# First scores of the attention between the last products of the projections, and two transfers moved behind the first key loads

## The chip, the cores and the metric

The kernel runs on one core of one Trainium2 chip. The metric is the device time of one execution in microseconds (us); the kernel before takes 1719.75 us as the median of three runs (1718.42 to 1723.87). The engines work at the same time and are tied to each other by semaphores: PE (TensorE) multiplies, DVE (VectorE) and ACT (ScalarE) read its results out of the PSUM banks, POOL (GpSimd) does element-wise work in SBUF, and SP (SyncE) issues the transfers. A transfer goes through one queue, in the order in which SP issues it.

## What is computed

One transformer block with modulated layer norms, attention over 32 heads of 16 columns, and a GELU layer, on 2048 rows of 512 columns in float32:

```python
mod = (silu(c) @ w_mod)            # six rows of 512: sa, ca, ga, sb, cb, gb
h = layernorm(x) * (1 + ca) + sa
qkv = h @ wqkv                      # q, k, v: 32 heads x 16 columns each
p = softmax((q @ k.T) * 16**-0.5)   # per head, 2048 x 2048
x = x + ga * ((p @ v) @ wo)
h = layernorm(x) * (1 + cb) + sb
x = x + gb * (gelu(h @ w1 + b1) @ w2 + b2)
```

The softmax is taken with the true maximum of each row, so every score is computed twice: once to find the row's maximum, once to take the exponential. Operands are split into an upper and a lower part, so that a product consists of several matrix multiplications.

## The kernel before, in words

**The stages.** A first stage (to about 69 us of the profile) normalises and transposes the four blocks `b` of 512 rows and makes the first products: the keys and queries of the first column group (`k = 0`) of each block, and some of the values. A second stage, the loop over `n` (L721 to L790), makes the other products (35 items: values, then keys and queries of column groups 1 to 3) with the row maxima of the first nine units woven in. A unit `u` is four heads times 512 rows of queries. The third stage, the loop over `s` (L1013 to L1035), is the attention: 32 units of 16 steps. A step has four scores (`X0` to `X3`, `exp_step`), each followed by an exponential on ACT, four products with the values (`P`, `pv_step`, of the step before), and three maxima of later units (`M`, `max_bank`). The last stage is the GELU layer.

**The first maxima.** In the second stage a maximum is found in pairs: `kd` holds for the key blocks 0 and 2 the keys themselves and for blocks 1 and 3 the difference to the block before. A `V` slot multiplies queries with the difference, ACT takes the relu (L579, tile `cp`), and a `U` slot multiplies the same queries with the keys; DVE adds both and keeps the extreme (L582). Each visit of the loop does one `V` and one `U`; about 0.68 visits fall on a step `i` of the loop. Units 0 and 1 take turns of eight slots: slots 0 to 7 use unit 0's queries with key blocks 0 and 1, slots 8 to 15 those of unit 1, and from slot 16 key blocks 2 and 3 are wanted.

**What feeds them.** `proj_qk` splits a product and hands back `rest`, which stores the parts to DRAM: `store(qk_d...)`, and for the keys of `k = 0` also `store(kd_d...)` (L464). `load_qm(u)` brings a unit's queries into a tile `qmx` by six transfers of 64 KB (L515); `build_k` brings keys into `kts[0]` by six transfers (L504). SP issues in the order of the program: at the start of block 3 it has the stores of block 2 (`qk`, `kd`, `qk`), then `load_qm(0)`, `build_k` for key blocks 0 and 1, `load_qm(1)`, then a store of values, the stores of block 3, and at `n = 0` `build_k` for key blocks 2 and 3. Eight semaphores go round over the transfers, so a transfer is issued only when the eighth before it has landed.

**The seam between the second and the third stage.** The product of an item is worked off in halves of 64 rows; the second half runs `LAG = 6` steps behind, so that for `n = N` (N = 35) and the first six steps of `n = N + 1` only second halves and maxima are left. `evacuate(N - 1)` copies the last product out (ACT, tile `raw`, L446). After that the pools of the stage are closed (`wcm`, `hcm`, `tcm`), the banks are dealt out anew (`set_rings`), `ppool` is opened, in whose tiles `p` the exponentials go, loads of keys are issued, and `epool` is opened with the loads of `ga_b` and `gb_b` (L812). Then step `s = 0` begins: `X0` to `X3` and no maxima.

**What sets the order.** All of this is written out by hand: each engine executes its instructions in the order of the program.

## Time and profile before

| | us |
|---|---|
| median of 3 runs | 1719.75 |
| lowest and highest run | 1718.42, 1723.87 |
| the profiled execution's own time | 1728.43 |
| its span, first to last instruction | 1726.7 |
| PE busy | 1715.8 |
| DVE busy | 1389.9 |
| ACT busy | 1352.9 |
| POOL busy | 312.7 |

The times of day in the text are us from the start of the span. A row of the timeline gives the start, the length, the engine, the line, the operation, the tile written and the tile read, and how many instructions were merged (`x6`); in brackets stands how long the engine idled before it and what ended that. `SPq` is SP issuing a transfer. A row of busy time by stretch gives for each engine the busy us and the number of instructions (`x`), then the clock that TensorE was granted (1.00 is full), the share of time in which the transfer engines were busy, and GB/s. PE's ends of matmuls are modelled, so that PE looks busy in nearly every stretch; how much it gets done is read from counts.

### The profile page before, as it was taken

Reading aid. Unit: us, or ns where it says so; the run is one execution under the profiler, and the core shown is the slowest. Engines: PE = TensorE matmul, PEld = TensorE weight load, DVE = VectorE, ACT = ScalarE, POOL = GpSimd, SP = SyncE. Lnnn points to the kernel's source line nnn. Section 1 sums busy time; section 2 is a strip of 40 time slices with the busy share of each in tenths; the row PEclk is TensorE's granted clock in tenths of the full one; section 3 lists DMA queues with packets and bytes.
Section 4 is the critical chain, followed back from the end, with each engine's and each line's share of the span. In section 5 each row is a group of like instructions: output and inputs, shape, how many; then the busy total and the mean of one; then the engine's idle time right before and its main releaser. Section 6 shows DMA issues by size and latency. Waiting matters only on the chain.

```text
span 1726.7 us, 29970 instructions
## 1 busy us (share of the span) xinstructions
PE 1715.8 (99%) x10968; PEld 905.6 (52%) x10968; DVE 1389.9 (80%) x2559; ACT 1352.9 (78%) x2580; POOL 312.7 (18%) x341
## 2 busy tenths in 40 slices
PE   9999999999999999999999999999999999999998
PEld 7766664333443334333433343334433488888887
DVE  6699997998888888888888888888885296746453
ACT  3588888999999999999999999999999632222222
POOL 3205430110000000000000000000022154636562
PEclk9899998999999999999999999999999999999999
DMA  9854988314112201400500110111023064423331
GB/s 328 223 124 153 172 177 162 73 41 60 40 36 44 55 24 33 69 23 24 88 23 23 43 33 24 39 32 27 23 66 106 19 204 131 138 79 110 99 122 49
DMA packets 125223, 144.22 MB, mean 84 GB/s; under 512 B 39026, under 2 KB 74866, under 8 KB 123124
## 3 DMA queue, kind: packets, MB, share of 16 engines
q1 hardware_dynamic: 123828, 139.71, 32.6%
q10 hardware_dynamic: 1248, 2.59, 0.4%
q8 instruction: 86, 1.41, 0.4%
q14 instruction: 61, 0.50, 0.1%
HBM read 106.37 MB, written 35.87 MB: 82 GB/s over the span
## 4 chain that ended last, share of the span: by engine, by line
PE 95%; DVE 2%; ACT 1%; SPq 1%; DMA 1%; issue 1%; POOL 0%; ACTq 0%
PE pv L843 30%; PE mx L554 20%; PE sc L1010 14%; PE sc L308 9%; PE mx L1074 6%; PE mx L573 5%; PE sc L776 4%; PE pv L1074 2%; PE sc L950 2%; PE sc L773 2%; PE mx L950 1%; PE sc L261 0%; PE sc L359 0%; DMA wmod<-in_w_mod_dram 0%; DVE bst L239 0%
## 5 line engine op out<-in xcount | busy, mean ns | idle before, releaser
L1011 ACT ACTIVATE p<-sc 128x512 f32<-128x512 f32 x2048 | 1054.7, 613 | 43.1 <-PE sc L1010 16.8
L556 DVE TENSOR_REDUCE mxs<-mx 128x1 f32<-128x512 f32 x1472 | 928.1, 683 | 118.8 <-PE sc L1010 91.4
L843 PE MATMUL pv<-p,vg 128*32 128x512 f32 x4096 | 548.1, 607 | 0.0
L1010 PE MATMUL sc<-qst,kq 50*128 50x512 f32 x1024 | 286.8, 438 | 0.3 <-ACT raw L446 0.3
L1010 PE MATMUL sc<-qst,kt 50*128 50x512 f32 x1024 | 282.5, 432 | 0.0
L554 PE MATMUL mx<-kq,qmx 48*128 48x512 f32 x768 | 262.5, 428 | 0.5 <-DVE mxs L556 0.4
L554 PEld LDWEIGHTS mx<-kq,qmx 48*128 48x128 f32 x768 | 121.9, 184 | 230.4 <-DVE mxs L556 212.1
L554 PE MATMUL mx<-kt,qmx 48*128 48x512 f32 x704 | 241.1, 430 | 0.0
L554 PEld LDWEIGHTS mx<-kt,qmx 48*128 48x128 f32 x704 | 113.6, 186 | 211.0 <-DVE mxs L556 191.5
L1053 ACT ACTIVATE g<-sc,b_c 128x512 f32<-128x512 f32 x56 | 38.6, 690 | 223.0 <-PE sc L308 218.5
L595 POOL CAST m<-mn 128x16 fp32r<-128x16 f32 x32 | 6.3, 198 | 1040.8 <-DVE mn L589 1040.8
L582 DVE CUSTOM_DVE_ANT_0 cp<-mx,cp 128x512 f32<-128x512 f32 x288 | 182.1, 686 | 14.0 <-PE mx L573 11.2
L573 PE MATMUL mx<-kt,qmx 48*128 48x512 f32 x576 | 181.1, 428 | 2.9 <-DMA qmx<-qk 1.2
L579 ACT ACTIVATE cp<-mx 128x512 f32<-128x512 f32 x288 | 157.2, 603 | 26.2 <-PE mx L573 20.9
L843 PEld LDWEIGHTS pv<-p,vg 128*32 128x32 f32 x4096 | 81.1, 108 | 181.3 <-issue 169.7
L1010 PEld LDWEIGHTS sc<-qst,kq 50*128 50x128 f32 x1024 | 126.8, 186 | 30.3 <-ACT p L1011 21.3
L573 PEld LDWEIGHTS mx<-kt,qmx 48*128 48x128 f32 x576 | 102.5, 190 | 57.7 <-DVE mxf L582 34.3
L1057 DVE TENSOR_TENSOR glo<-g,ghi 128x512 fp32r<-128x512 f32 x56 | 57.6, 1029 | 92.1 <-ACT ghi L1056 92.1
L1010 PEld LDWEIGHTS sc<-qst,kt 50*128 50x128 f32 x1024 | 125.6, 185 | 9.4 <-ACT p L1011 2.4
L879 POOL TENSOR_TENSOR w1l<-w1r,w1h 128x512 fp32r<-128x512 f32 x56 | 76.5, 1366 | 146.7 <-DVE w1h L878 123.1
L881 POOL TENSOR_TENSOR w2l<-w2r,w2h 128x512 fp32r<-128x512 f32 x56 | 82.5, 1473 | 6.2 <-DVE w2h L880 5.8
L308 PE MATMUL sc<-kt,w1h 128*128 128x512 f32 x224 | 73.8, 391 | 0.0
(185 smaller groups left out, 1912.5 us busy)
## 6 DMA issues: line engine op xcount, KB each, us to landing
qk<-parts SPq DMA_DIRECT2D x30, 512.0 KB
w1r<-in_B_w_dram SPq DMA_DIRECT2D x56, 256.0 KB
w2r<-in_B_w_dram SPq DMA_DIRECT2D x56, 256.0 KB
qmx<-qk SPq DMA_DIRECT2D x192, 64.0 KB
qst<-qk SPq DMA_DIRECT2D x192, 64.0 KB
kq<-qk SPq DMA_DIRECT2D x24, 256.0 KB
kt<-qk SPq DMA_DIRECT2D x24, 256.0 KB
vg<-v SPq DMA_DIRECT2D x8, 664.0 KB
```

What stands on the lines that cost most here:

```text
L308: te.matmul(ps, p, q, start=i == 0, stop=i == len(terms) - 1)
L554: te.matmul(ps, qmx[u][rows, p, qc * P : (qc + 1) * P], kst[u // NB][rows, p, kr * TB : (kr + 1) * TB], start=True, stop=True)
L556: ve.tensor_reduce(mxs[u][:, p, a, qc, kr : kr + 1], ps, axis=AX.X, op=ALU.max, negate=True)
L573: te.matmul(ps, qmx[u][rows, p, qc * P : (qc + 1) * P], kd[u // NB][rows, p, t0 : t0 + TB], start=True, stop=True)
L579: ac.activation(vpos[n, a], ps, AF.Relu)
L582: ve.tensor_tensor_reduce(v, ps, v, -1.0, 3.0e38, ALU.add, ALU.min, mxs[u][:, p, a, qc, r : r + 1])
L843: te.matmul(cur_pv[0][32 * j : 32 * (j + 1)], vg[g][:, kc, j * VW : j * VW + 32], pt.pop((s, j)), start=kc == 0, stop=kc == NKC - 1)
L879: gp.tensor_tensor(alo, a, ahi.bitcast(F32), op=ALU.subtract)
L881: gp.tensor_tensor(blo, b, bhi.bitcast(F32), op=ALU.subtract)
L1010: te.matmul(ps, k[r0 : r0 + KX, p, kc * P : (kc + 1) * P], q[r0 : r0 + KX, p], start=True, stop=True)
L1011: ac.activation(pb, ps, AF.Exp, scale=SCALE)
L1074: te.matmul(acc[qb][t], p[:, sl], q, start=f == 0 and n == 0, stop=f == NF - 1 and n == 2)
```

## The change

Front: the store of block 2's keys to `kd_d[0]` is kept in a list `late` and issued with block 3's keys; `load_qm(1)` is taken from before the second stage to `n = 0`, ahead of the second `build_k`.

Seam: the four scores and exponentials of attention step 0 are issued inside the second stage's last two rounds, at steps 9 and 11 of `n = N` and steps 1 and 3 of `n = N + 1`. The tiles of `ppool` don't exist yet there, so these four go to a new tile `px` and to three tiles of the projections that are free by then (`pm`, two halves of `wraw`). Because of this `tcm` is closed later: `epool` is opened, with its two loads, after attention step 1. The bank of the last product is taken out of the ring, and the rings are dealt out in another order. Step 0 of the attention loop then issues no scores.

```diff
+FIRST_X = (9, 11, 13, 15)
...
         def rest():
             store(qk_d[w][k], parts)
-            if pair and b % 2 == 0:
+            if pair and b == 2 and not k:
+                late.append(lambda: store(kd_d[k], parts))
+            elif pair and b % 2 == 0:
                 store(kd_d[k], parts)
             elif pair:
+                while late and not k:
+                    late.pop(0)()
...
             load_qm(0)
             build_k(kts[0], kd_d[0], 0, 0, 2 * TB)
-            load_qm(1)
...
         if n == 0:
+            load_qm(1)
             build_k(kts[0], kd_d[0], 0, 2 * TB, S)
...
+        if n == N:
+            wraw = tpool.tile([P, 2, KC, P], F32, tag="wraw", name="p_w", bufs=1).rearrange("p a k n -> p a (k n)")
+            pm = tpool.tile([P, TB], F32, tag="pm", name="p_m", bufs=1)
+            pxcm, pxpool = pool("pxpool")
+            px = pxpool.tile([P, TB], F32, name="px")
+            first_p.extend([px, pm, wraw[:, 0], wraw[:, 1]])
...
                 acc[n] = bank()
+                if n == N - 1:
+                    last_sc = rings["sc"].pop()
...
+            if n >= N and (n - N) * NT + i in FIRST_X:
+                exp_step(0, FIRST_X.index((n - N) * NT + i))
...
-    close(tcm)
...
-    set_rings(sc=(sc[0], sc[1], mx[0], sc[2]), mx=mx[1:4], pv=mx[4:])
+    set_rings(sc=(sc[0], mx[0], sc[1], last_sc), mx=mx[1:4], pv=mx[4:])
...
-    epool = ctx.enter_context(tc.tile_pool(name="epool", bufs=1, side="right"))
+    def open_epool():
+        nonlocal epool, wo_hi, wo_lo, x2a, b2_b, ga_b, gb_b, o_b, xn_b
+        close(tcm)
+        epool = ctx.enter_context(tc.tile_pool(name="epool", bufs=1, side="right"))
...
+    at(1, open_epool)
...
             if tok[0] == "X":
-                exp_step(s, int(tok[1]))
+                if s:
+                    exp_step(s, int(tok[1]))
```

`exp_step` itself is moved up in the file and takes its tile from `first_p` for step 0. `build_k` loses an unused argument.

More of the change, by code (lines that the diff above doesn't have):

```diff
@@ L311, in block_kernel @@
     st = [ac]
+    late = []
     def first_block():
@@ L497, in heads, with build_k @@
         return ap.rearrange("(p a d) t -> a d p t", a=2, d=DH)[a]
-    def build_k(dst, src, g, t0=0, t1=S, parts=(0, 1, 2)):
-        for i in parts:
+    def build_k(dst, src, g, t0=0, t1=S, eng=sy):
+        for i in range(3):
             part = (0, 0, 1)[i]
@@ L503, in build_k @@
                 r0 = a * 64 + i * DH
-                sy.dma_start(dst[r0 : r0 + DH, :, t0:t1].bitcast(F32), heads(src, g, part, a, t0, t1))
+                eng.dma_start(dst[r0 : r0 + DH, :, t0:t1].bitcast(F32), heads(src, g, part, a, t0, t1))
     def load_k(g, tile):
@@ L540, in one_rows, with exp_step @@
             sy.dma_start(k[r0 : r0 + 2].bitcast(F32), one_d[:, None, :].to_broadcast([2, 2, S]))
+    pt, first_p = {}, []
+    def exp_step(s, j):
+        u, kc = divmod(s, NKC)
+        q, k = qst[u], kst[u // NB]
+        p, a = divmod(j, 2)
+        ps = bank()
+        pb = pt[s, j] = ppool.tile([P, TB], F32, tag="p", name="p", bufs=10) if s else first_p[j]
+        r0 = a * 64
+        te.matmul(ps, k[r0 : r0 + KX, p, kc * P : (kc + 1) * P], q[r0 : r0 + KX, p], start=True, stop=True)
+        ac.activation(pb, ps, AF.Exp, scale=SCALE)
     mxs, left, vpos = {}, {}, {}
@@ L702, in block_kernel @@
     led, todo = 0, []
-    new, late = [], []
+    new = []
     def visit():
@@ L804, in block_kernel @@
     load_k(3, kq[1])
-    epool = ctx.enter_context(tc.tile_pool(name="epool", bufs=1, side="right"))
-    wo_hi = epool.tile([P, KC, D], FR, name="wo_hi")
-    wo_lo = epool.tile([P, KC, D], FR, name="wo_lo")
-    x2a = [epool.tile([P, 4, D], F32, name=f"x2a{i}") for i in range(2)]
-    b2_b, ga_b, gb_b = [epool.tile([P, D], F32, name=n) for n in ("b2_b", "ga_b", "gb_b")]
-    for i, t in enumerate((ga_b, gb_b)):
-        sy.dma_start(t, bass.AP(tensor=g_d.tensor, offset=g_d[i].offset, ap=[[0, P], [1, D]]))
-    o_b = epool.tile([P, 4, D], F32, name="o_b")
-    xn_b = epool.tile([P, 4, D], F32, name="xn_b")
+    epool = wo_hi = wo_lo = x2a = b2_b = ga_b = gb_b = o_b = xn_b = None
+    def open_epool():
+        nonlocal epool, wo_hi, wo_lo, x2a, b2_b, ga_b, gb_b, o_b, xn_b
+        close(tcm)
+        epool = ctx.enter_context(tc.tile_pool(name="epool", bufs=1, side="right"))
+        wo_hi = epool.tile([P, KC, D], FR, name="wo_hi")
+        wo_lo = epool.tile([P, KC, D], FR, name="wo_lo")
+        x2a = [epool.tile([P, 4, D], F32, name=f"x2a{i}") for i in range(2)]
+        b2_b, ga_b, gb_b = [epool.tile([P, D], F32, name=n) for n in ("b2_b", "ga_b", "gb_b")]
+        for i, t in enumerate((ga_b, gb_b)):
+            sy.dma_start(t, bass.AP(tensor=g_d.tensor, offset=g_d[i].offset, ap=[[0, P], [1, D]]))
+        o_b = epool.tile([P, 4, D], F32, name="o_b")
+        xn_b = epool.tile([P, 4, D], F32, name="xn_b")
     wo_r = {}
@@ L823, in wo_load @@
             sy.dma_start(b2_b, bass.AP(tensor=b2.tensor, offset=b2.offset, ap=[[0, P], [1, D]]))
-    pt = {}
     def attn_out(u, pv):
@@ L1000, in block_kernel @@
         at(base + n, lambda i=i: run("l", lambda: ln2(0), i))
-    def exp_step(s, j):
-        u, kc = divmod(s, NKC)
-        q, k = qst[u], kst[u // NB]
-        p, a = divmod(j, 2)
-        ps = bank()
-        pb = pt[s, j] = ppool.tile([P, TB], F32, tag="p", name="p", bufs=10)
-        r0 = a * 64
-        te.matmul(ps, k[r0 : r0 + KX, p, kc * P : (kc + 1) * P], q[r0 : r0 + KX, p], start=True, stop=True)
-        ac.activation(pb, ps, AF.Exp, scale=SCALE)
     for s in range(NS):
@@ L1036, in block_kernel @@
     pv_step(NS - 1)
-    for cm in (pcm, qcm, vgcm, kqcm, qmcm):
+    for cm in (pcm, pxcm, qcm, vgcm, kqcm, qmcm):
         close(cm)
```

## The prediction

> **What bounds the kernel now.** First the page: busy time, the slices with the granted clock, the chain that ended last by engine.

> ```profile
> span 1726.7 us, 29970 instructions
> ...
> PE 1715.8 (99%) x10968; PEld 905.6 (52%) x10968; DVE 1389.9 (80%) x2559; ACT 1352.9 (78%) x2580; POOL 312.7 (18%) x341
> ...
> PEclk9899998999999999999999999999999999999999
> ...
> PE 95%; DVE 2%; ACT 1%; SPq 1%; DMA 1%; issue 1%; POOL 0%; ACTq 0%
> ```

> PE ends nearly all of the chain, so time is lost where PE waits or runs slowly. The clock line has three slices that aren't 9: the start, the second (43 to 86 us) and the seventh (259 to 302 us). The change touches just these last two places. Busy time by stretch, cut where the granted clock changes (columns: stretch, length, then PE, PEld, DVE, ACT and POOL busy with instruction counts, clock, transfer share, GB/s):

> ```profile
> 67.41:70.82 3.41, 2.25 (x10) 1.34 (x9) 0.69 (x1) 1.46 (x4) 1.73 (x2) 1.00 0.92 140
> 70.83:84.47 13.64, 13.64 (x52) 11.24 (x51) 7.84 (x23) 8.17 (x15) 0.00 (x0) 0.50 0.89 228
> 84.48:98.12 13.64, 13.43 (x104) 9.16 (x103) 12.82 (x41) 11.96 (x23) 0.00 (x0) 1.00 0.40 109
> 265.39:268.79 3.40, 3.10 (x16) 1.33 (x15) 2.29 (x10) 3.40 (x8) 1.72 (x4) 1.00 0.79 290
> 268.80:279.03 10.23, 10.23 (x45) 3.88 (x37) 5.27 (x9) 5.84 (x12) 0.52 (x1) 0.50 0.92 152
> 279.04:289.27 10.23, 10.23 (x75) 3.97 (x73) 8.83 (x14) 9.57 (x19) 0.00 (x0) 1.00 1.02 117
> ```

> Two stretches run at half clock, 13.64 and 10.23 us long. They are 4 and 3 times 3.41 us, and they begin 197.97 us apart, which is 58 times 3.413: the clock seems to be set on a fixed grid of 3.41 us. In the grid cell before each of them PE did little: 10 matmul records in 3.41 us and 16 in 3.40, against 104 in 13.64 (26 per cell) behind the first. The relu copies of the first stretch, alone:

> ```profile
> 84.48:98.12 13.64, 11.21 (x21) 1.00 0.40 109
> ```

> In the half-clock stretch all 15 ACT instructions are such copies, so it made 15 where an equal time at full clock makes 21: worth 15/21 × 13.64 = 9.74 us, a loss of 3.9. The second made 12 exponentials against 19 behind it: worth 12/19 × 10.23 = 6.46, a loss of 3.8.

> **Front: the wait before the first maximum.** PE's and SP's rows:

> ```profile
> 68.18 0.73 PE L773 MATMUL sc<-wv,hThi 64*128 64x512 f32 x2
> 70.06 0.47 PE L573 MATMUL mx<-kt,qmx 48*128 48x512 f32 x1 [1.16 <-DMA qmx<-qk]
> ...
> 55.36 0.46 SPq L464 DMA_DIRECT2D kd<-parts  x1
> 55.92 0.87 SPq L464 DMA_DIRECT2D qk<-parts  x1
> 56.88 4.29 SPq L515 DMA_DIRECT2D qmx<-qk  x6
> 61.21 3.98 SPq L504 DMA_DIRECT2D kt<-kd  x6
> 65.23 3.77 SPq L515 DMA_DIRECT2D qmx<-qk  x6
> 69.79 0.35 SPq L488 DMA_DIRECT2D v<-vst  x1
> ...
> 70.81 0.46 SPq L464 DMA_DIRECT2D kd<-pmh  x1
> ...
> 75.07 2.67 SPq L504 DMA_DIRECT2D kt<-kd  x6
> ```

> The profile names a query transfer, but by the program the first maximum needs unit 0's queries (from 56.88) and five of the six key transfers (from 61.21). The value store at 69.79 can be issued only when the fifth key transfer, eight before it, has landed; so the keys end the wait.

> *The store of block 2's keys* (55.36) goes from in front of them. Its size and the rate there:

> ```profile
> kd<-parts SPq DMA_DIRECT2D x1, 512.0 KB
> ...
> 56.00:60.00 4.00, 4.00 (x19) 3.23 (x18) 2.81 (x6) 2.31 (x4) 1.46 (x2) 1.00 1.02 367
> 62.00:70.00 8.00, 6.90 (x27) 4.12 (x25) 2.67 (x4) 3.83 (x7) 2.52 (x2) 1.00 1.02 150
> ```

> 512 KB at 367 GB/s are 1.4 us, with the transfer engines busy throughout; the keys come that much earlier, at 68.7 instead of 70.06. PE is there at 68.18 + 0.73 = 68.91. I leave 0.15 us for the sixth transfer: gain 1.0, bounds 0 (SP's issue is held by something else) and 1.16.

> *Unit 1's queries* (65.23) stood behind the keys, so moving them gains nothing there, and no more than the rest of the wait. They now stand behind a value store and three stores of 512 KB. The second keys were issued when the last of these had landed, at 75.07; the later stream is 1.4 us longer by the moved store and shorter by what left its front, so I put that landing at 75; six transfers of 64 KB at the 150 GB/s of the row above take 2.6 more: 77.6. Wanted they are at slot 8, the 17th visit: 16 visits at 21 per 13.64 us are 10.4, so at 79.3. Margin 1.7 us. The second keys follow, six transfers in at most the 8 us of the row above, at 86; wanted at slot 16, 20.8 us after 68.9, at 89.7. Both hidden; uncovered they would cost their lateness.

> *The slow stretch* that follows the wait should go with it: 3.9. Bounds 0 and 3.9.

> **Seam.**

> ```profile
> 265.20 0.40 PE L1010 MATMUL sc<-qst,kq 50*128 50x512 f32 x1
> 265.89 1.96 PE L1010 MATMUL sc<-qst,kq 50*128 50x512 f32 x4 [0.30 <-ACT raw L446]
> 268.27 1.48 PE L843 MATMUL pv<-p,vg 128*32 128x512 f32 x8
> ...
> 260.91 2.75 ACT L579 ACTIVATE cp<-mx 128x512 f32<-128x512 f32 x5
> 264.00 0.60 ACT L579 ACTIVATE cp<-mx 128x512 f32<-128x512 f32 x1 [0.33 <-PE mx L573]
> 265.24 0.60 ACT L446 ACTIVATE raw<-sc 128x512 f32<-128x512 f32 x1 [0.65 <-PE sc L776]
> 265.74 4.02 ACT L1011 ACTIVATE p<-sc 128x512 f32<-128x512 f32 x8
> ...
> 265.93 0.69 DVE L582 CUSTOM_DVE_ANT_0 cp<-mx,cp 128x512 f32<-128x512 f32 x1
> ```

> The eight exponentials of steps 0 and 1 follow each other without a gap, 4.02/8 = 0.50 us each, and PE's scores go at that pace with no values between: that is the thin cell. The change moves four of them, 2.0 us, among the copies from 260.91 on. No work goes away; ACT's idle 0.33 + 0.65 is filled: gain 1.0. Bounds: 2.0 gain (all four beside other work) and 2.0 loss (they delay copies for which DVE, which has no idle time up to 265.93, must wait); the idle rows are nearest. The first values still wait for DVE's last extreme, so they start at about 266.8 instead of 268.27, and PE's cells hold four scores more before, and values earlier. Then the clock doesn't fall: 3.8. Bounds 0 and 3.8.

> *Small edits.* `ga_b` and `gb_b` now wait for the first values on SP; behind them stand `vg` and the queries for unit 10, wanted tens of steps later, and these loads were held up to 288.50 before:

> ```profile
> 288.50 0.34 SPq L812 DMA_DIRECT2D ga_b<-g  x1
> ```

> `px`, `pm`, `wraw` have no reader left; the order of rings only says which bank is freed first, and the last product's copy is issued later than now by some exponentials, but its store feeds a late unit. Zero.

> **Sum.** 1.0 + 3.9 + 1.0 + 3.8 = 9.7. Against the profiled execution: 1728.43 − 9.7 = 1718.7. The median is 8.7 below that execution, nearly as much as both slow stretches (7.7). Either the unprofiled runs lack them, or profiling costs something in each. The three runs lie 1.3 and 4.1 apart, and 4.1 is about one stretch. I take it that the median run has one of the two, the third run both: 1719.75 − 2.0 − 3.85 = 1713.9.

> [...]

> **Rivals.**
> 1. *Both stretches are in every run*, and the 8.7 is the cost of profiling: 1719.75 − 9.7 = 1710.0. For it: their cause, a wait and a paced chain, is the same in each run.
> 2. *Only the waits go*: the clock of the median run isn't slow before, or still falls after, as a grid cell may lie over what is left thin: 1719.75 − 2.0 = 1717.7. For it: 8.7 against 7.7. Against: a cause that repeats.
> 3. *The transfers aren't what held the keys*, and the exponentials only change places: 1719.7.
> 4. *Slower: unit 1's queries come late.* PE stops at slot 8 and the clock falls there. With lateness w it costs w + 3.9 − 2.0; it decides from a landing of 79.3 on, and passes 0.3% at w = 3.3, a landing at 82.6: 1725. Against: the margin of 1.7.

> **How the numbers follow.** 0.3% (5.2 us; below it a measurement of this kernel can't be told from no change) is 1714.6. Forecast 0.42, own range 1712 to 1716, two thirds of it faster; rival 1 0.20; rival 2 0.22; rival 3 0.06; rival 4 0.10. Faster 0.28 + 0.20 = 0.48; within 0.14 + 0.22 + 0.06 = 0.42; slower 0.10. Range 1709.5 to 1720: it takes in rivals 1 to 3 and leaves out the last, and what lies below the first.

> **What would show it.** Clock 1.00 from 5 us to 1700; PE's idle time before its first maximum below 0.3 us; ACT without gaps from the first `px` to the exponentials of step 2; values of successive steps 2.1 us apart from step 0 on. Wrong would be: a half-clock stretch near 70 or 262, a wait of PE for `qmx` near 79, DVE idle near 263 for want of copies, or an after-profile without slow stretches whose runs are no faster.

## The result and the profile after

The changed kernel takes 1716.74 us as the median of 20 runs (1715.77 to 1717.55). The kernel before, run beside it, takes 1724.22 (20 runs, 1718.42 to 1728.77). The ratio is 0.9958 with a 95% interval of 0.9949 to 0.9966: faster by 0.42%. The profiled execution took 1716.99 us, against 1728.43 before: 11.44 us less. These two executions lie further apart than the medians, 7.48, because the one before was among its slowest.

The page of the changed kernel, the same lines as before:

```profile
span 1715.2 us, 29972 instructions
...
PE 1705.7 (99%) x10968; PEld 899.2 (52%) x10968; DVE 1389.4 (81%) x2559; ACT 1351.7 (79%) x2580; POOL 312.4 (18%) x341
...
PEclk9999999999999999999999999999999999999999
...
PE 96%; DVE 3%; ACT 1%; issue 1%; POOL 0%; ACTq 0%; POOLq 0%; DVEq 0%
```

DVE and ACT are busy as long as before to within 1.2 us, PE 10.1 us less with the same count of matmuls: the same products took less time. Both half-clock slices are gone from the clock line (there were two, the second and the seventh; the start, which the prediction counts too, is a 9 in the line before). Busy time by stretch of the changed kernel, cut as before:

```profile
67.41:70.82 3.41, 3.41 (x18) 2.57 (x17) 0.69 (x1) 2.85 (x6) 1.93 (x2) 1.00 1.07 391
70.83:84.47 13.64, 13.43 (x97) 9.34 (x96) 13.21 (x43) 12.07 (x24) 0.00 (x0) 1.00 0.97 207
...
259.22:262.62 3.40, 3.21 (x19) 1.39 (x19) 2.77 (x9) 3.17 (x7) 1.99 (x4) 1.00 0.86 319
```

Where 10 and 52 matmuls stood before, there are now 18 and 97. The front in PE's and SP's rows of the changed kernel (L804 was L773, L595 was L573):

```profile
68.37 0.73 PE L804 MATMUL sc<-wv,hThi 64*128 64x512 f32 x2
68.83 0.51 PE L595 MATMUL mx<-kt,qmx 48*128 48x512 f32 x2
...
60.13 2.75 SPq L513 DMA_DIRECT2D kt<-kd  x6
63.00 0.35 SPq L497 DMA_DIRECT2D v<-vst  x1
...
65.41 0.46 SPq L468 DMA_DIRECT2D kd<-parts  x1
...
68.59 4.67 SPq L524 DMA_DIRECT2D qmx<-qk  x6
74.05 1.24 SPq L513 DMA_DIRECT2D kt<-kd  x3
```

The keys are issued from 60.13 (61.21 before), the moved store stands at 65.41 behind them, and the first maximum follows without a wait. The seam in the rows of ACT, DVE and PE (L562 is the exponential, L601 the relu copy):

```profile
254.10 1.09 ACT L601 ACTIVATE cp<-mx 128x512 f32<-128x512 f32 x2
255.05 0.63 ACT L562 ACTIVATE px<-sc 128x512 f32<-128x512 f32 x1
255.53 1.14 ACT L601 ACTIVATE cp<-mx 128x512 f32<-128x512 f32 x2
...
259.34 2.22 ACT L562 ACTIVATE p<-sc 128x512 f32<-128x512 f32 x4
261.80 2.06 ACT L562 ACTIVATE p<-sc 128x512 f32<-128x512 f32 x4 [0.23 <-PE sc L561]
...
259.48 0.69 DVE L604 CUSTOM_DVE_ANT_0 cp<-mx,cp 128x512 f32<-128x512 f32 x1
...
260.24 0.62 PE L878 MATMUL pv<-px,vg 128*32 128x512 f32 x1
...
262.86 1.06 PE L878 MATMUL pv<-p,vg 128*32 128x512 f32 x8
...
265.00 1.06 PE L878 MATMUL pv<-p,vg 128*32 128x512 f32 x8
```

**Where the 11.44 us went**, between the two profiled executions. The first maximum comes at 68.83 instead of 70.06: 1.23. DVE's last extreme before the attention comes at 259.48 instead of 265.93: 6.45, so 5.2 more were gained between 70 and 266, where the first half-clock stretch was. The other 5.0 were gained at the seam, its ACT gaps and the second half-clock stretch together.

### The profile page after: what moved, and what is told of

It is laid out like the page before. It is cut to its first block, busy times and chain, and to the rows that moved or that the text cites. A ratio compares the mean times of both kernels' runs of the same rounds, so it can differ in the third digit from the quotient of the medians.

```text
span 1715.2 us, 29972 instructions
## 1 busy us (share of the span) xinstructions
PE 1705.7 (99%) x10968; PEld 899.2 (52%) x10968; DVE 1389.4 (81%) x2559; ACT 1351.7 (79%) x2580; POOL 312.4 (18%) x341
## 4 chain that ended last, share of the span: by engine, by line
PE 96%; DVE 3%; ACT 1%; issue 1%; POOL 0%; ACTq 0%; POOLq 0%; DVEq 0%
PE pv L878 30%; PE mx L576 20%; PE sc L561 14%; PE sc L310 9%; PE mx L1100 6%; PE mx L595 5%; PE sc L807 3%; PE pv L1100 2%; PE sc L986 2%; PE sc L804 2%; PE mx L986 1%; DVE cp L604 1%; PE sc L263 0%; PE pv L350 0%; PE sc L363 0%
## 5 line engine op out<-in xcount | busy, mean ns | idle before, releaser
L562 ACT ACTIVATE p<-sc 128x512 f32<-128x512 f32 x2044 | 1053.0, 615 | 39.9 <-PE sc L561 14.0
L576 PE MATMUL mx<-kt,qmx 48*128 48x512 f32 x704 | 239.9, 427 | 0.1
L595 PE MATMUL mx<-kt,qmx 48*128 48x512 f32 x576 | 176.1, 416 | 1.8 <-ACT cp L601 1.0
L601 ACT ACTIVATE cp<-mx 128x512 f32<-128x512 f32 x288 | 156.8, 604 | 19.7 <-PE mx L595 13.5
L595 PEld LDWEIGHTS mx<-kt,qmx 48*128 48x128 f32 x576 | 100.3, 184 | 57.6 <-DVE mxf L604 35.3
## 6 DMA issues: line engine op xcount, KB each, us to landing
qk<-parts SPq DMA_DIRECT2D x30, 512.0 KB
```

The costliest lines, as they stand in the source:

```text
L562: ac.activation(pb, ps, AF.Exp, scale=SCALE)
L576: te.matmul(ps, qmx[u][rows, p, qc * P : (qc + 1) * P], kst[u // NB][rows, p, kr * TB : (kr + 1) * TB], start=True, stop=True)
L595: te.matmul(ps, qmx[u][rows, p, qc * P : (qc + 1) * P], kd[u // NB][rows, p, t0 : t0 + TB], start=True, stop=True)
L601: ac.activation(vpos[n, a], ps, AF.Relu)
```

## The experiments

All times are medians with the lowest and highest run. Fill means products that nobody reads; they use the identity tile `ident` or go to a bank `idle`. The clock of a run is its mean granted clock; one grid cell of 3.41 us (the half-clock stretches of 13.64 and 10.23 us before are four and three of them) at half clock takes 3.41/2/1726 = 0.001 from it, so that the mean clock counts the cells also where a run has no trace.

My theory: thin work of PE in one cell of the 3.41 us grid costs the clock, and the clock is most of the time. Rivals: the waits and the exponentials' order cost the time themselves; or a gap of about 1 us loses the clock wherever it lies.

**1. The front part alone** (kernel before):

```diff
-            if pair and b % 2 == 0:
+            if pair and b == 2 and not k:
+                held.append(lambda: store(kd_d[k], parts))
+            elif pair and b % 2 == 0:
...
+                while held and not k:
+                    held.pop(0)()
...
-            load_qm(1)
...
+            load_qm(1)
             build_k(kts[0], kd_d[0], 0, 2 * TB, S)
```

> The kernel before with the front part of the change alone: block 2's key store and unit 1's queries moved, the seam as it was. Theory (each place loses a wait, and then a half-clock stretch whenever a 3.41 us cell of the clock's grid lies over the thin part): PE's idle time before its first maximum is under 0.3 us and the clock stays 1.00 there; the seam still has its half-clock stretch of 3 or 4 cells in most runs, so the time is 1716.7 + 1.0 (ACT's gaps) + 4 to 5 = 1721 to 1723 in these, and 1718 where the grid misses it. Rival (the clock has nothing to do with the two places; the gain is the shorter waits and the order of work): half-clock stretches would come in the front as before, and the time would lie 1 us below the kernel before.

Measured: 1719.26 (1716.32 to 1724.26, 12 runs), ratio 0.9986 (0.9973 to 1.0000). The kernel before had 1723.45 in the 33 runs beside it. The interval reaches 1, so the time alone doesn't show a gain. The first maximum and the stretches at the seam:

```profile
67.88 0.61 PE L578 MATMUL mx<-kt,qmx 48*128 48x512 f32 x2
...
257.90:261.31 3.41, 3.11 (x15) 1.33 (x15) 2.30 (x8) 3.41 (x8) 1.94 (x4) 1.00 0.52 190
261.32:274.96 13.64, 13.64 (x56) 5.22 (x52) 7.03 (x11) 7.67 (x16) 0.30 (x1) 0.50 0.96 147
```

The front's wait and half clock are gone, and the seam's half clock stays, here for four cells after a cell of 15 matmuls. The runs go from 1716.32 at a clock of 0.999 to 1724.26 at 0.995; I had expected 1718 where the grid misses the seam, and four of the twelve lie below that.

**2. The seam part alone**: the changed kernel with the two transfers put back.

> The kernel before with the seam part alone: scores of step 0 between the last products, the front as it was. Theory: the wait of about 1.2 us before the first maximum is back, with a half-clock stretch behind it in about half of the runs, none at the seam: 1717.9 without and 1722 to 1723 with the stretch. Rival (order of work alone): 1 us below the kernel before, with half-clock stretches at the seam as before.

Measured: 1717.19 (1716.34 to 1723.08, 12 runs), ratio 0.9978 (0.9964 to 0.9992), in two groups: seven runs from 1716.34 to 1717.48, all at a clock of 1.000, and five from 1720.50 to 1723.08 at 0.996 to 0.997. The profiled execution (1716.34), at full clock until its last 3 us, still has the front's wait:

```profile
68.90 0.47 PE L590 MATMUL mx<-kt,qmx 48*128 48x512 f32 x1 [0.69 <-DMA qmx<-qk]
```

So runs with this wait and the full clock are as fast as the changed kernel; what the other five lose comes with the clock.

**3. Fill in both places of the kernel before**: five 128x128 identity products on PE ahead of the first maximum, and one ahead of each score of steps 0 and 1, into the score's own bank.

```diff
+            if n == 1 and i == 1:
+                idle = bank_mx()
+                for _ in range(5):
+                    te.matmul(idle[:, :P], ident, ident, start=True, stop=True)
...
+        if s < 2:
+            for _ in range(1):
+                te.matmul(ps[:, :P], ident, ident, start=True, stop=True)
         te.matmul(ps, k[r0 : r0 + KX, p, kc * P : (kc + 1) * P], q[r0 : r0 + KX, p], start=True, stop=True)
```

> The kernel before, no work moved; five multiplications of the identity by itself are put before the first maximum, to be done while PE waits there, and one before each of the eight scores of attention steps 0 and 1. They compute nothing that is used. Theory (it is PE's thin activity in a cell of the grid that costs the clock): no half-clock stretch in either place, and the time is 1716.7 + 1.0 to 1.2 (wait) + 1.0 (ACT's gaps) = 1718.5 to 1719, with a spread of about 2 us between runs. Rival (late keys and the order of work are the cost): as slow as the kernel before or slower by up to 1 us, with its spread of 10 us.

Measured: 1727.52 (1725.69 to 1731.29, 10 runs), slower than before by a ratio of 1.0041 (1.0025 to 1.0057): a miss. In the profile the front kept its clock, but at the seam fill and scores took turns, 0.42 us each, so that scores came 0.84 us apart instead of 0.50, and three cells of half clock followed. The fill made the seam longer and hardly fuller (0.39 of the cell ahead of the fall instead of 0.34, counted as in the table behind run 11). Run 6 tries the seam's fill again, with a bank of its own.

**4. Unit 1's queries later**: the changed kernel, with `load_qm(1)` behind the second `build_k`.

```diff
         if n == 0:
-            load_qm(1)
             build_k(kts[0], kd_d[0], 0, 2 * TB, S)
+            load_qm(1)
```

> The changed kernel with unit 1's queries issued behind the second keys instead of ahead of them. Theory (a late tile costs its lateness, and then the clock): the queries land near 82 to 83 instead of 75.4, wanted at about 79; PE stops for 2 to 4 us, and a half-clock stretch of 4 cells follows in most runs: 1716.7 + 3 + 4 to 5 = 1723 to 1725, 1720 where the clock holds. Rival (the clock doesn't follow waits): 1720 in all runs. If 1717, the tile is wanted later than I reckoned.

Measured: 1722.38 (1721.32 to 1723.20, 12 runs), 5.6 more than the changed kernel.

```profile
82.63 0.79 PE L595 MATMUL mx<-kt,qmx 48*128 48x512 f32 x2 [4.51 <-DMA qmx<-qk]
...
76.96:80.36 3.40, 1.16 (x9) 0.33 (x5) 1.59 (x6) 1.26 (x3) 0.00 (x0) 1.00 1.02 121
80.37:87.20 6.83, 4.57 (x22) 3.93 (x24) 2.34 (x7) 2.11 (x4) 0.00 (x0) 0.50 0.87 207
```

This is what my slower rival described, at the place it named: a wait of 4.51 us at slot 8, and the clock falls in the next cell, for two cells. The cost is less than the wait and the two cells (up to 1.7 us each) add up to; what made good the rest is not shown. In the changed kernel the queries are issued from 68.59 on, and PE doesn't wait there.

**5. The seam part with fill in front**: run 2's kernel and the five identity products of run 3.

> The kernel before with the seam part alone, and five 128x128 identity products put on PE ahead of the first maximum, where it waits for the keys (the wait itself stays). The seam part alone gave two groups, 1716.3 to 1717.5 at a clock of 1.0 and 1720.5 to 1723.1 at 0.996 to 0.997. Theory, it is the thin work of PE in one 3.41 us cell that loses the clock: the second group goes, all runs 1716.3 to 1718 at a clock of 0.999 or more, no half-clock stretch near 70. Rival, the wait itself or what comes behind it loses the clock: both groups stay, median about 1717 with runs above 1720.

Measured: 1718.12 (1716.69 to 1719.33, 6 runs), ratio 0.9965 (0.9951 to 0.9979). All at a clock of 0.999 or more and none above 1720, as the theory wanted; but three runs, 1718.50 to 1719.33, lie above the 1718 that I had as its limit. Their spans from first to last instruction are 1716.1 to 1716.4, at a clock of 0.999 or more, so these three lost time outside the span. By chance alone six runs would all fall among run 2's seven of twelve at full clock about once in 25 times, so this supports the theory without settling it.

**6. The front part with fill at the seam in a bank of its own**:

```diff
+    idle = []
...
+        if s < 2:
+            if not idle:
+                idle.append(bank_mx())
+            te.matmul(idle[0][:, :P], ident, ident, start=True, stop=True)
```

> The kernel before with the front part alone, and one 128x128 identity product ahead of each of the eight scores of steps 0 and 1, this time into a bank of its own, so that a score does not wait for it. The front part alone had 4 cells of half clock at the seam in its profile and runs from 1716.3 to 1724.3. Theory (thin cells): the products add 0.2 to 0.3 us of PE work to each 0.50 us between two scores; no half-clock stretch near 262, all runs 1716.5 to 1719 at 0.999 or more. Rival (the seam's order of exponentials is itself the cost): a half-clock stretch stays and runs still reach 1722 and more. If the scores again come more than 0.6 us apart, the control is spoilt.

Measured: 1726.86 (1724.18 to 1733.72, 12 runs), ratio 1.0019 (1.0006 to 1.0032). PE's rows and the stretches:

```profile
259.09 0.49 PE L1020 MATMUL mx<-ident 128*128 128x128 f32 x2
259.50 0.50 PE L1021 MATMUL sc<-qst,kq 50*128 50x512 f32 x1
259.93 0.49 PE L1020 MATMUL mx<-ident 128*128 128x128 f32 x2
260.35 0.49 PE L1021 MATMUL sc<-qst,kq 50*128 50x512 f32 x1
...
258.80:262.20 3.40, 3.40 (x14) 1.90 (x12) 2.02 (x8) 2.27 (x4) 1.33 (x4) 1.00 1.03 378
262.21:272.43 10.22, 10.22 (x29) 4.97 (x30) 1.72 (x3) 3.50 (x7) 0.91 (x1) 0.50 0.93 170
```

The control is spoilt again: the bank wasn't the reason, a 128*128 product between two scores of 50 rows makes each wait 0.42 us for the other. But the row of the cell teaches something: PE has no idle time in its records there (3.40 of 3.40, with ends that are modelled), and still the clock falls. Idle time in the records isn't what decides.

**7 and 8. Which of the two transfers**: the changed kernel with only the store moved (7), and with only the queries moved (8), as in run 1's diff.

> The changed kernel with unit 1's queries loaded where they were, so that of the front only the store of block 2's keys is moved. Theory, the 512 KB store held the keys: the first maximum stands at 68.4 to 68.9 with a wait under 0.3 us, all runs 1716 to 1717.6 at a clock of 0.999 or more, as the changed kernel. Rival, the six query loads issued behind the keys share the queues and hold them: a wait of 0.6 to 1.2 us stays, and runs above 1720 with it.

> The changed kernel with the store of block 2's keys where it was, so that of the front only unit 1's queries are moved. Theory (the store held the keys): the first maximum waits 0.5 to 1.2 us as with the seam part alone, and a group of runs at 1720 to 1723 is there. Rival (the loads behind the keys held them): no wait, all runs 1716 to 1717.6 at 0.999 or more.

Measured: 1716.45 (1716.15 to 1716.76, 6 runs) with the store, 1717.02 (1716.56 to 1717.91, 6 runs) with the queries; clocks of 0.999 or more in both. First maximum with the store, then with the queries:

```profile
68.49 0.47 PE L595 MATMUL mx<-kt,qmx 48*128 48x512 f32 x1
```

```profile
68.26 0.70 PE L590 MATMUL mx<-kt,qmx 48*128 48x512 f32 x2 [0.43 <-DMA v<-vst]
```

With the store alone moved, no wait is left, as I had it. The second part of my theory missed: with the queries alone the wait is 0.43 us, and no run lost the clock. Moving the queries isn't needed for the time. Whether moving the store is, six runs can't tell: that none of run 8's lost the clock would come by chance once in 25 times, as in run 5. Nor do single profiles tell the wait's size well: with neither transfer moved it was 1.16 us in the kernel before and 0.69 in run 2.

**9. The front part with fill of the scores' own shape**: the scores whose operands lie in partitions 0 to 63 (`a` is 0) are made three times, the first two into a bank of their own.

```diff
+    idle = []
...
+        if s < 2 and not a:
+            if not idle:
+                idle.append(bank_mx())
+            for _ in range(2):
+                te.matmul(idle[0], k[:KX, p, kc * P : (kc + 1) * P], q[:KX, p], start=True, stop=True)
```

> The kernel before with the front part alone, and each score of steps 0 and 1 that uses the lower 64 rows of the array made three times, the first two into a bank of their own: the fill is of the scores' own shape, so it should not push them apart as the identity products did (0.42 us each). Theory (thin cells): the scores stay 0.50 us apart, the cell ahead of 262 us holds more work, no half-clock stretch there, all runs 1716.3 to 1718.5 at 0.999 or more, where the front part alone reached 1724.3. Rival (the order of the exponentials is itself the cost): half clock stays near 262, runs up to 1724. If the scores again come more than 0.6 us apart, the control is spoilt.

Measured: 1716.15 (1715.86 to 1717.57, 11 runs) at 0.999 or more, ratio 0.9967 (0.9954 to 0.9979).

```profile
259.72:263.12 3.40, 3.40 (x26) 1.63 (x28) 2.19 (x5) 3.32 (x8) 2.06 (x4) 1.00 0.72 267
...
256.62 0.60 ACT L584 ACTIVATE cp<-mx 128x512 f32<-128x512 f32 x1 [0.34 <-PE mx L578]
257.87 0.60 ACT L447 ACTIVATE raw<-sc 128x512 f32<-128x512 f32 x1 [0.65 <-PE sc L781]
258.36 12.04 ACT L1023 ACTIVATE p<-sc 128x512 f32<-128x512 f32 x23
```

The exponentials of the first steps follow each other in one block behind the same two ACT gaps as in the kernel before, and PE makes products that nobody reads; yet it is as fast as the changed kernel. In 12 runs without this fill (run 1) the time reached 1724.26. So at the seam neither the order of the exponentials nor ACT's gaps are worth anything that can be seen here: what the order is worth is the clock.

**10. Gaps in the dense part**: the changed kernel with 15 gaps in the feed-forward part, made by small copies on ACT that PE waits for (`gap` is a tile that holds the identity).

```diff
+        if i % 4 == 2 and i < 60:
+            te.matmul(ps[:, :P], gap, gap, start=True, stop=True)
+            for _ in range((3, 6, 9)[i // 4 % 3]):
+                ac.activation(gap, ident, AF.Copy)
+            te.matmul(ps[:, :P], gap, gap, start=True, stop=True)
```

> The changed kernel with 15 gaps of PE in the feed-forward part, where its products use the whole array without a break: every fourth product of the first layer waits for 3, 6 or 9 small copies on ACT in turn, gaps of about 1, 2 and 3 us. Theory (the work in a 3.41 us cell decides, and cells filled to under about 0.38 lose the clock): the cells here are filled to 0.94, so a gap of up to 1.9 us within a cell costs no clock, and only gaps of more than 2.0 us that lie in one cell are followed by half clock. So none after the five shortest, some after the five longest. Rival (a gap of about 1.2 us, as ahead of the first maximum, loses the clock by itself): half clock after the shortest too.

Measured by its profile (its time, 1770.08, is the gaps'; 14 of them stand out in the records). Two waits, and the cells of three gaps, each with what follows:

```profile
1386.38 0.49 PE L1082 MATMUL sc<-gap 128*128 128x128 f32 x2 [1.08 <-ACT gap L1081]
...
1503.64 0.49 PE L1082 MATMUL sc<-gap 128*128 128x128 f32 x2 [2.10 <-ACT gap L1081]
...
1384.70:1388.10 3.40, 2.32 (x13) 1.83 (x12) 3.33 (x7) 0.93 (x3) 2.85 (x2) 1.00 0.84 272
1388.11:1391.50 3.39, 3.39 (x16) 2.80 (x15) 1.35 (x4) 1.32 (x2) 3.28 (x4) 1.00 0.49 135
1500.73:1504.14 3.41, 1.31 (x8) 1.03 (x7) 3.04 (x6) 1.86 (x6) 3.30 (x3) 1.00 0.44 132
1504.15:1507.56 3.41, 3.41 (x9) 2.66 (x9) 0.00 (x0) 0.00 (x0) 2.71 (x3) 0.50 0.42 126
1592.90:1596.30 3.40, 1.91 (x9) 1.65 (x10) 2.72 (x8) 1.31 (x5) 2.91 (x3) 1.00 0.94 283
1596.31:1599.72 3.41, 3.41 (x17) 2.82 (x15) 0.68 (x2) 1.32 (x2) 1.80 (x2) 1.00 0.75 226
```

None of the five gaps of 1.08 us cost the clock. Of the three of 2.10 us one did, the one in the rows at 1500.73, which lies in a single cell; the one before 1594.39 lies over two cells and did not, nor did the third, at 1669, which lies mostly in one. All six longer ones did. In the kernel before a wait of 1.16 us, and one of 0.30 us, had been followed by half clock. So a gap doesn't decide by its length.

**11. Fill alone**: the kernel before with nothing moved, with the fill of run 5 in front and that of run 9 at the seam.

> The kernel before with nothing moved: five 128x128 identity products on PE in the wait ahead of the first maximum, and the lower scores of steps 0 and 1 made three times (16 fill products in all, 8 of them of the scores' shape twice over). Both waits stay. Theory (nearly all of the gain is the clock, and thin cells cost it): all runs 1716.2 to 1718.5 at 0.999 or more, within 1 us of the changed kernel's 1716.74, and no half-clock stretch near 70 or 262. Rival (the waits that the change removes are worth about 2 us, as my prediction had them): 1718 to 1719.5 at the same clock. Rival (the clock falls with the waits whatever fills the cells): runs at 1720 to 1726 as before.

Measured: 1718.20 (1717.43 to 1719.14, 12 runs), all at 0.999 or more, ratio 0.9977 (0.9967 to 0.9986). The 17 runs of the kernel before beside it had 1723.06. Thirteen products that nobody reads (five in front, eight at the seam; the expectation's sixteen is a slip), and no order changed, give 4.9 us. The time lies 1.5 above the changed kernel's 1716.74, where I had expected less than 1, and two runs lie above 1718.5. The 1.5 would be the waits, which stay, and the fill itself: the first maximum comes at 69.74, 0.91 later than in the changed kernel, and the rest isn't taken apart. The second theory's range (1718 to 1719.5) holds the median too: the waits are worth something, but it is the small part.

**What a thin cell is.** From the matmul records of all 13 profiles I worked out how full each cell was: the streaming time of each record (0.227 us for 512 columns at full clock, the distance between successive records in the dense part, 12 of them from 1499.90 to 1502.62 in the changed kernel; twice that for operands that the kernel keeps as `F32` and not as `FR`: in the kernel before, the value products, which start in fours, stand 0.45 us apart, at 279.26 and 279.72, and 16 records of the identity, 128 columns each, start 0.11 us apart from 1380.73 on), times the share of 128*128, the largest shape in the records, that its own shape covers (64*128 is a half), summed and divided by 3.413 (197.97/58, from the two falls of the kernel before).

| cells that began at full clock | filled to |
|---|---|
| the 13 followed by half clock | 0.03, 0.04, 0.17, 0.27, 0.31, 0.31, 0.32, 0.34, 0.37, 0.38, 0.39, 0.39, 0.39 |
| the fullest of these, by run | runs 1, 3 and 6 0.39, run 10 0.38, before 0.37 (front) and 0.34 (seam) |
| the lowest of the others (some 6450) | 0.41 (run 10), 0.42 (run 8), 0.44 (run 5), 0.46 (runs 7 and 2) |

The program's last cells, where the work runs out, are left out. The fill sorts all cells, with the border between 0.39 and 0.41; that is a narrow margin, as some records may be missing. PE's busy time doesn't sort the cells (lost with 3.40 of 3.40 in run 6, kept with 1.91 in run 10), nor does the count of matmuls (lost with 16, kept with 9). The streaming time without the shape's share doesn't either: counted so, run 1's lost cell is filled to 1.32, more than one product at a time, and the cell at 1592.90 in run 10, which kept the clock, to 0.53. With the share of the rows alone run 1's cell comes to 1.04, with that of the columns alone to 0.68. So of the counts tried only the one with the whole shape's share sorts all cells; what the chip itself counts is not shown.

The cells behind a fall sort in the same way. With the streaming time doubled (in the kernel before, at a clock of 0.50, the fours of the value products stand 0.85 us apart, at 271.68 and 272.53), the 14 half-clock cells that were followed by another are filled to 0.28 to 0.76, and the 13 that ended a half-clock stretch to 0.79 to 1.06. In products done that is a border between 0.38 and 0.40, beside 0.39 and 0.41 at full clock.

## Why the prediction was right, and which steps were wrong

The measured 1716.74 lies in the range, and "faster" had the largest chance. The mechanism was right: most of the time lay in two half-clock stretches behind two thin cells, and the change removes both. Part of the success is luck: 1716.74 lies above my own range of 1712 to 1716 and above 1714.6, below which I counted "faster". It is faster because the kernel before, run 20 times, has a median of 1724.22 and not 1719.75. The steps:

- **Store and keys: right.** Keys at 68.7, PE there at 68.91, an idle time under 0.3; measured 68.83 and none. Run 7 shows that moving the store is enough.
- **Moved loads hidden: right.** PE has no wait near 79 or 90. Run 4 shows what they would have cost uncovered.
- **Seam: right in place.** I had the first values 1.47 earlier by the order alone. They stand at 260.24 instead of 268.27, 8.03 earlier; less the 6.45 gained before, that is 1.6. Values of successive steps stand 2.62 and 2.14 apart, not 2.1 from the first on, and ACT keeps one gap of 0.23.
- **Waits, 1.0 + 1.0: too large.** Of the 82 runs of the kernel before that stand beside the experiments (33, 16, 16 and 17), seven stood at a clock of 1.000, with both waits in the program: 1716.97 to 1718.47, median 1717.64, 0.9 above the changed kernel. The seam's 1.0 for ACT's idle 0.33 + 0.65 is the one that fails: run 9 has 0.34 and 0.65 still and takes 1716.15.
- **Stretches, 3.9 + 3.8: too small.** Over those 82 runs the time rises by 1.53 us per 0.001 of mean clock, which is one cell. Seven cells make 10.7; with the waits' 0.9 that is 11.6 against the 11.44 found. My step compared 15 copies with the 21 of the stretch behind it, but the pace that the half clock held back was higher. The changed kernel makes 23 in the same 13.64 us, of which 15 are worth 8.9, a loss of 4.7:

```profile
70.83:84.47 13.64, 11.69 (x23) 1.00 0.97 207
```

- **The step that failed: "1719.75 − 2.0 − 3.85".** The sum against the profiled execution gave 1718.7, the time of a kernel without either stretch, and no run can lose more than it has. Taking one stretch off a median that holds fewer half-clock cells gave 1713.9, below every run of every kernel here (1715.77 is the lowest). I had read 1719.75 as "one stretch": it was a low draw of three. In the 82 runs 63 are above 1720, and the median is 1723.49, some four cells above the floor. So I should have forecast the floor: 1718.7 by my sizes, and 1728.43 − 11.6 = 1716.8 by the sizes measured here.
- **The first rival's premise, a cost of profiling of 8.7, is refuted**: the profiled 1716.99 lies among the other runs, 1715.77 to 1717.55. The second rival's 1717.7 came nearer than my forecast, but for a wrong reason: it left the clock as it was.
- **Gaps and the clock.** None of run 10's five gaps of 1.08 us in dense work cost the clock. But half clock followed 0.30 us of idle time in the kernel before, none in the records of run 6, and 2.10 us in run 10: it is a question of the whole cell, filled to 0.39 or less in each of these falls.

The spread of the kernel before, 1716.90 to 1730.14 at clocks from 1.000 to 0.992, would follow if the grid lay differently over the thin places in each run. Runs without a trace can't show this, so it stays argued.

## What to carry to other kernels

Look for half-clock stretches in the granted clock and at the 3.41 us cell ahead of each: if PE's products there fill it as little as in the 13 lost cells here (0.39 or less), fill that cell, by moving work into it (1716.74 here) or with products nobody reads, of the same tile shape as their neighbours (1716.15 in run 9; with 128*128 products among 50-row scores 1726.86 in run 6). A wide spread of runs that goes with the mean clock is itself the sign (here 1716.90 to 1730.14, 1.53 us per 0.001), and the fastest run at full clock tells the floor that such a repair can reach (here 1716.97 before the change, 1716.74 as the median after it). Forecast that floor, not the median less the sum.
